# A transform run in smaller portions among matrix products, and an intermediate reordered by its copy

## The chip, the cores and the metric

The kernel runs on one core of a Trainium2 chip. The metric is the device time in microseconds (us). A kernel is run several times, and the median is quoted with the lowest and the highest time.

Engine names in the profile: PE is the tensor engine, PEld its weight loads, DVE the vector engine, ACT the scalar engine, POOL is GpSimd. In the traces below an engine takes its instructions in the order of the built program (run 1 shows ACT doing so). SBUF is the on-chip memory, and PSUM the memory into which PE writes.

## The reference, cut to what matters

The function is the forward and backward pass of a gated sum. One branch multiplies a two-dimensional real Fourier transform by complex weights, the other is a two-layer network with a squared ReLU. S is 2048, D is 1024, F is 3584, the data are bf16. It returns the output and eight gradients.

```python
X = rfft2(x.astype(float32)) * (w_r + 1j * w_i)
a = irfft2(X, s=(S, D)).astype(bfloat16)
h = einsum("bsd,df->bsf", x2, w1) + b1
r = where(h > 0, h, 0)
b = einsum("bsf,fd->bsd", r * r, w2) + b2
g = sigmoid((x * gate_w).sum(-1, keepdims=True))
out = g * a + (1 - g) * b          # jax.vjp(out)(grad_out) gives the eight gradients
```

## The kernel before

PE does everything large: 5376 products of 128x512 (six groups of 896) for the network, and the transforms, which are written as small matmuls. The transform of x and the transform of the output's gradient go through the same instructions as T = 0 and T = 1. The program is written as two generators, which a helper interleaves: for each 16-product accumulation of the weight gradients (`pw`; I call one such accumulation a *slot*) the transform generator is moved on by some steps. A step ends at a `yield`. What is left of the transform runs at one step per 28-product accumulation (`acc`) of the output stage. There DVE multiplies each finished accumulator with `go`, a loaded tile of the output's gradient, and sums the result into `bGo`; only then is the accumulator free again.

```python
def spread(main, side, per_main, start=0.0):
    due, done = start, 0
    for _ in main:
        due += per_main
        while done < due:
            next(side, None)
            done += 1
        yield
...
spec, grads = spectra(), mlp_grads()          # spectra: fft_mid, then fft_out
next(grads), next(grads)
todo = 1 + 6 * (S2 // 2) + NT                 # S2 // 2 = 8 pairs, NT = 16 tiles
for _ in spread(grads, spec, todo / (2.0 * FG * FGC * NH - 2)):
    pass
for _ in mlp_out():                           # 32 accumulations
    next(spec, None)
```

The middle of the transform (`fft_mid`) takes eight pairs of 128-point columns. A pair has two *units* (j) for each T: three matmuls, two into a PSUM buffer `px` and one into `pxs`; ACT copies `pxs` to SBUF as `common`; DVE adds it to both halves of `px`. `back` has the same form with `pv`, `pvs` and `v`. Each kind of PSUM buffer exists twice.

```python
def spectrum(fb, T, m, z, mats):
    ...                                       # DVE forms pm and sums
    for j in range(2):
        px = fps.tile([P, 2, H], FP32, name="px", tag="ps2", bufs=2)
        ps = tps.tile([P, H], FP32, name="pxs", tag="tr", bufs=2)
        mm(px[:, 0, :], lhsT=mats[:, j, 1, :], rhs=im, start=True, stop=True)
        mm(px[:, 1, :], lhsT=mats[:, j, 2, :], rhs=re, start=True, stop=True)
        mm(ps[:], lhsT=mats[:, j, 0, :], rhs=sums[:, j], start=True, stop=True)
        common = fb.tile([P, H], FP32, name="common", tag="common", bufs=2)
        nc.scalar.copy(out=common[:], in_=ps[:])
        by_l = lambda ap: ap.rearrange("p c (g i) -> p c i g", g=4)
        V(out=x[:, j, :, 0:H].rearrange("p c (i g) -> p c i g", g=4), in0=by_l(px[:]),
          in1=by_l(common[:]...).to_broadcast([P, 2, P, 4]), op=ALU.add)

# fft_mid, for each pair m
for T in range(2):
    xs.append(spectrum(fb, T, m, z[:, T], am))
    yield
real_columns(...)                             # small matmuls "sp"
for T in range(2):
    ...                                       # DVE: y = x * w, four products, combined
    yield
back(fb, m, y, ap)                            # all four units in one step
yield
...                                           # DVE: the gradient of the weights, gs
nc.scalar.mul(out=gw[:, :, :, 0:W1], in_=gs[:, :, :, 0:W1], mul=GS)
...
yield

# fft_out, for each of 32 tiles
...                                           # eight matmuls into pki
rt = fb.tile([P, 8, P], FDT, name="rt", tag="rt", bufs=2)
nc.scalar.copy(out=rt[:], in_=pk[:])
pu = fps.tile([P, 2, H], FP32, name="pui", tag="ps2", bufs=2)
column_stage(INV, pu, rt, ci)                 # eight matmuls into pui, from rt
...                                           # ACT copies pui, DVE finishes, store
yield 2
```

`spread` does not read the value that a generator yields, so `yield 2` is one step.

## Time and profile before

| | before |
|---|---|
| time, median of three | 1351.44 us (1350.59 to 1353.70) |
| span of the profiled execution | 1351.5 us |
| PE, DVE, ACT busy | 98%, 61%, 31% |
| PE idle, 450 to 800 us (transform among weight gradients) | 8.3 us |
| PE idle, 800 to 1060 us (last transform stage) | 3.3 us |
| PE idle, 1060 to 1100 us (start of the output stage) | 2.5 us |

The idle times are the length of a stretch less PE's busy time in it. They understate what is lost, because the end of a PE record is modelled: a record of 0.38 us stands for 0.216 us of issue. So in the tables further down I count another way, from the trace of one execution of each kernel: the distance between the starts of two neighbouring PE instructions, less N/2.4 ns + 2.5 ns for N columns (the prediction checks this spacing against the trace), for each distance that is over 30 ns too long. It is put down to the stage of the second instruction. Where a PE record is missing, the weight loads, whose records are all there, tell how many; this leaves an uncertainty of a few tenths of a us. This *lost PE time* is 11.6 us for the middle of the transform, 7.8 us for the last stage, and 2.6 us for the stop near 1075 us, plus 1.7 us for a stretch of half clock that follows it.

### The profile page before, as it was taken

The numbers are of one execution on the slowest core, as the hardware profiler recorded it, in microseconds if no ns is written. First come the engines' busy times: TensorE is split into PE (matmuls) and PEld (weight loads), VectorE is DVE, ScalarE is ACT, GpSimd is POOL, SyncE is SP. The second block draws the span as 40 slices with busy tenths as digits, with TensorE's granted clock in tenths as the row PEclk, the third lists the DMA queues.
The fourth block names the chain that finished last, engine by engine and source line by source line (L and its number), as shares of the span: only waits on it lengthen the run. The fifth ranks groups of instructions, "written<-read, shape, count | busy, mean of one in ns | idle before, by whom it ended". The sixth has DMA issues, their size and how long they took to land. (4 is left out here: it accounts for less than half of the span.)

```text
span 1351.5 us, 18838 instructions
## 1 busy us (share of the span) xinstructions
PE 1322.1 (98%) x7082; PEld 637.1 (47%) x7082; DVE 824.3 (61%) x1541; ACT 418.4 (31%) x658; POOL 299.3 (22%) x484
## 2 busy tenths in 40 slices
PE   7999999999999999999999999999999999999998
PEld 5644444444444444444444445454545444444443
DVE  7966667666565696769666782233856565642222
ACT  6854555555433323332233223343212000000000
POOL 0222223222322254443433222111101000000000
PEclk9999999999999999999999999999999999999999
DMA  8558778786778979889776548666888754653530
GB/s 280 188 182 250 255 229 259 247 252 225 226 235 242 287 226 196 202 234 200 206 167 194 141 126 276 208 220 233 214 224 230 203 169 133 193 165 94 155 102 24
DMA packets 217093, 273.31 MB, mean 202 GB/s; under 512 B 16988, under 2 KB 152170, under 8 KB 217002
## 3 DMA queue, kind: packets, MB, share of 16 engines
q1 hardware_dynamic: 181306, 153.84, 42.9%
q0 software_dynamic: 35696, 118.27, 27.0%
q8 instruction: 55, 0.90, 0.3%
q14 instruction: 36, 0.29, 0.1%
HBM read 147.25 MB, written 118.51 MB: 197 GB/s over the span
## 5 line engine op out<-in xcount | busy, mean ns | idle before, releaser
L617 PE MATMUL ph<-xT,w1g 128*128 128x512 bf16 x896 | 218.5, 381 | 2.0 <-ACT rT L619 1.7
L627 PE MATMUL pd<-dbT,w2T 128*128 128x512 bf16 x896 | 212.3, 379 | 1.2 <-DVE dhT L631 0.5
L904 PE MATMUL acc<-w,hblk 128*128 128x512 bf16 x896 | 199.8, 381 | 2.4 <-DVE bGo L906 2.4
L838 PE MATMUL pw<-grd,res 128*128 128x512 bf16 x896 | 201.6, 379 | 0.0
L821 PE MATMUL pw<-dbn,grp 128*128 128x512 bf16 x896 | 200.4, 379 | 0.0
L946 PE MATMUL accg<-w1Tr,hblk 128*128 128x512 bf16 x896 | 193.7, 379 | 0.0
L946 PEld LDWEIGHTS <-hblk 128*128 128x128 bf16 x896 | 87.6, 98 | 106.3 <-issue 0.9
L627 PEld LDWEIGHTS <-w2T 128*128 128x128 bf16 x896 | 87.2, 98 | 104.9 <-issue 1.6
L821 PEld LDWEIGHTS <-grp 128*128 128x128 bf16 x896 | 86.9, 98 | 105.4 <-issue 2.4
L904 PEld LDWEIGHTS <-hblk 128*128 128x128 bf16 x896 | 87.5, 98 | 103.3 <-issue 4.9
L838 PEld LDWEIGHTS <-res 128*128 128x128 bf16 x896 | 86.4, 98 | 101.3 <-issue 3.0
L617 PEld LDWEIGHTS <-w1g 128*128 128x128 bf16 x896 | 86.9, 98 | 99.5 <-issue 2.8
L619 ACT ACTIVATE rT<-ph,b1col 128x512 bf16<-128x512 f32 x112 | 77.0, 687 | 145.1 <-PE ph L617 145.0
L631 DVE SCALAR_TENSOR_TENSOR dhT<-pd,rT 128x512 bf16<-128x512 f32 x112 | 75.2, 671 | 65.9 <-PE pd L627 58.6
L951 DVE TENSOR_TENSOR gxo<-accg,g 128x512 bf16<-128x512 f32 x32 | 22.1, 690 | 108.1 <-PE accg L946 107.9
L736 DVE STREAM_TRANSPOSE stg<-h2T 128x512 int32<-128x512 int32 x56 | 39.8, 711 | 73.7 <-ACT h2T L620 73.7
L825 ACT CAST wo<-pw 128x512 bf16<-128x512 f32 x56 | 32.7, 585 | 156.6 <-PE pw L821 145.6
L833 POOL DMA_DIRECT2D out_dram<-wo x112 | 56.7, 514 | 84.8 <-ACT wo L825 79.1
L843 ACT CAST wo<-pw 128x512 bf16<-128x512 f32 x56 | 32.8, 586 | 125.7 <-PE pw L838 122.7
L620 ACT ACTIVATE h2T<-rT 128x512 bf16<-128x512 bf16 x112 | 70.6, 630 | 3.1
L743 DVE STREAM_TRANSPOSE stgd<-dhT 128x1024 bf16<-128x1024 bf16 x56 | 69.3, 1238 | 1.3
L496 DVE TENSOR_TENSOR ev<-e 128x256 f16<-128x256 f16 x32 | 9.3, 289 | 93.5 <-ACT e L493 93.4
(174 smaller groups left out, 1494.2 us busy)
## 6 DMA issues: line engine op xcount, KB each, us to landing
h2T_scr<-h2T POOLq DMA_DIRECT2D x28, 512.0 KB, 4.5
h_scr<-stg POOLq DMA_DIRECT2D x28, 512.0 KB, 7.0
dhT_scr<-dhT POOLq DMA_DIRECT2D x28, 512.0 KB, 8.0
dh_scr<-stgd POOLq DMA_DIRECT2D x28, 512.0 KB, 6.9
grp<-h_scr SPq DMA_DIRECT2D x112, 128.0 KB
grd<-dh_scr SPq DMA_DIRECT2D x112, 128.0 KB
hblk<-h2T_scr SPq DMA_DIRECT2D x8, 1792.0 KB
hblk<-dhT_scr SPq DMA_DIRECT2D x8, 1792.0 KB
```

What stands on the lines that cost most here:

```text
L617: mm(ph[:], lhsT=w1g[:, dc, fc % 2 * P : (fc % 2 + 1) * P], rhs=xT[:, dc, ss], start=(dc == 0), stop=(dc == DC - 1))
L619: nc.scalar.activation(rT[:], ph[:], ACT.Relu, bias=b1col[:, fc : fc + 1])
L620: nc.scalar.activation(h2T, rT[:], ACT.Square)
L627: mm(pd[:], lhsT=w_[:, ec // 2, ec % 2 :: 2], rhs=dbT[:, ec, ss], start=(ec == 0), stop=(ec == DC - 1),)
L631: return STT(out=dhT, in0=pd[:], scalar=2.0, in1=rT[:], op0=ALU.mult, op1=ALU.mult, accum_out=gb1part[:, fc, sb : sb + 1],)
L736: nc.vector.transpose(out=stg[:, :, c, :], in_=h2T[:, c, :].bitcast(I32).rearrange("p (b i) -> p b i", i=32))
L743: nc.vector.transpose(out=stg[:, :, :, c, :].rearrange("p b k i -> p k b i"), in_=dhT[:, c, :].rearrange("p (k b i) -> p k b i", b=4, i=32),)
L821: mm(pw[:], lhsT=cur[:, t // 2, 2 * fb_ * P + t % 2 : 2 * (fb_ + 1) * P : 2], rhs=dbn[:, t, hf * H : (hf + 1) * H], start=(t == 0), stop=( ...
L833: st(out=dst[q], in_=wo[32 * q : 32 * (q + 1), :])
L838: mm(pw[:], lhsT=xr[t][:, d_ * P : (d_ + 1) * P], rhs=cur[:, t], start=(t == 0), stop=(t == NT - 1),)
L904: mm(acc[:], lhsT=cur[:, fc, t2::2], rhs=w2[:, fc, cs], start=(fc == 0), stop=(fc == FC - 1))
L946: mm(acc[:], lhsT=cur[:, fc, t2::2], rhs=w1T[:, fc, 2 * hf : 2 * hf + 2, :], start=(fc == 0), stop=(fc == FC - 1),)
```

## The change

The intent is to give each engine time between portions, so that PE does not stand before a PSUM buffer that is still being emptied. Each unit becomes a step of its own, and each half of a last-stage tile. Since there are now more steps, the number of steps per slot is raised. And ACT writes `common` in the order in which DVE reads it, so DVE reads one of its two sources without hops.

```diff
-    def spectrum(fb, T, m, z, mats):
+    def spectrum(fb, m, z, mats, x):
@@
-            nc.scalar.copy(out=common[:], in_=ps[:])
-            by_l = lambda ap: ap.rearrange("p c (g i) -> p c i g", g=4)
+            nc.scalar.copy(
+                out=common[:].rearrange("p (i g) -> p i g", g=4), in_=ps[:].rearrange("p (g i) -> p i g", g=4)
+            )
             V(
-                out=x[:, j, :, 0:H].rearrange("p c (i g) -> p c i g", g=4), in0=by_l(px[:]),
-                in1=by_l(common[:].rearrange("p (o l) -> p o l", o=1)).to_broadcast([P, 2, P, 4]), op=ALU.add,
+                out=x[:, j, :, 0:H].rearrange("p c (i g) -> p c i g", g=4), in0=px[:].rearrange("p c (g i) -> p c i g", g=4),
+                in1=common[:].rearrange("p (o i g) -> p o i g", o=1, g=4).to_broadcast([P, 2, P, 4]), op=ALU.add,
             )
-        return x
+            yield
@@ back, at the end of each unit
+                yield
@@ fft_mid
-                xs.append(spectrum(fb, T, m, z[:, T], am))
-                yield
+                xs.append(fb.tile([P, 2, 2, LW], FDT, name=f"x{T}", tag=f"x{T}"))
+                yield from spectrum(fb, m, z[:, T], am, xs[T])
@@
-            back(fb, m, y, ap)
+            yield from back(fb, m, y, ap)
@@ fft_out
                 nc.scalar.copy(out=rt[:], in_=pk[:])
+                yield
                 pu = fps.tile([P, 2, H], FP32, name="pui", tag="ps2", bufs=2)
@@
-    todo = 1 + 6 * (S2 // 2) + NT
+    todo = 1 + 12 * (S2 // 2) + 2 * NT
```

Lines move by one or two: the products of the weight gradients are L821 and L838 before, L823 and L840 after; the output products L904 before, L906 after; the copy and the add of `spectrum` are L328 and L330 before, L327 and L330 after. In `back` the copy and the add are L381 and L382 in both.

More of the change, by code (lines that the diff above doesn't have):

```diff
@@ L318, in spectrum @@
         V(out=sums[:], in0=re_, in1=im_, op=ALU.add)
-        x = fb.tile([P, 2, 2, LW], FDT, name=f"x{T}", tag=f"x{T}")
         for j in range(2):
```

## The prediction

> **What bounds the kernel now.** I read the page's busy shares first, then busy time by stage, then what TensorE (PE) waits for, then single gaps in order of time, then the vector engine's (DVE) groups and the chain that ended last.
>
> ```profile
> PE 1322.1 (98%) x7082; PEld 637.1 (47%) x7082; DVE 824.3 (61%) x1541; ACT 418.4 (31%) x658; POOL 299.3 (22%) x484
> ```
>
> PE is busy for 98% of the span, so the time can only fall by what PE loses between its instructions. By stage (transforms among the weight gradients, 450 to 800; last transform stage, 800 to 1060; a gap, 1060 to 1100; the rest):
>
> ```profile
> 450.00:800.00 350.00, 341.73 (x1621) 153.17 (x1619) 263.94 (x340) 99.74 (x158) 128.80 (x231) 1.00 0.76 194
> 800.00:1060.00 260.00, 256.71 (x1505) 130.16 (x1504) 131.44 (x411) 84.98 (x100) 41.98 (x76) 1.00 0.77 224
> 1060.00:1100.00 40.00, 37.55 (x167) 16.63 (x166) 24.49 (x48) 0.00 (x0) 2.16 (x4) 0.96 0.76 209
> 1100.00:1350.00 250.00, 247.54 (x1143) 111.33 (x1140) 101.60 (x140) 0.00 (x0) 12.19 (x21) 1.00 0.43 128
> ```
>
> The columns are stretch, length, then busy us of PE, PE's weight loads, DVE, ACT and GpSimd, granted clock, DMA share, GB/s. PE is idle 8.3, 3.3 and 2.5 us in the three stretches that the change touches. DVE is at 75% in the first and blocks nothing for long. What PE waited for:
>
> ```profile
> PE pvs L379 <- ACT common L381: 3.6, 3, 1.2
> PE pv L377 <- DVE v L382: 2.8, 4, 0.7
> PE acc L904 <- DVE bGo L906: 2.4, 1, 2.4
> ...
> PE px L325 <- DVE pm L311: 1.6, 2, 1.2
> PE pxs L326 <- DVE sums L318: 0.8, 2, 0.4
> ```
>
> The first two are waits for a PSUM buffer: four units (two T, two j) of the backward transform stand almost together in PE's order, with two buffers of each kind. The third unit needs the buffers that the first unit's copy and add have yet to free:
>
> ```profile
> 677.84 0.38 PE L379 MATMUL pvs<-ysums,apmat 128*128 128x512 f16 x1
> 678.06 0.38 PE L821 MATMUL pw<-dbn,grp 128*128 128x512 bf16 x1
> 679.68 0.38 PE L379 MATMUL pvs<-ysums,apmat 128*128 128x512 f16 x1 [1.24 <-ACT common L381]
> ```
>
> Starts of dense 512-column matmuls are 0.216 us apart (39 in 8.58 us elsewhere, one record being 0.38), so a start at 678.28 was due and 1.40 us went, of which the record shows 1.24. Each gap hides 0.38 - 0.216 = 0.16 us in this way. The eleven waits of the transform stage (3+4+2+2) sum to 8.8 us idle, so to 8.8 + 11 x 0.16 = 10.6 us of PE time.
>
> In the last stage each of the 32 tiles has a shorter gap of the same kind:
>
> ```profile
> 860.32 0.61 PE L487 MATMUL pki<-ki,r 128*128 128x128 f16 x8
> 860.76 1.67 PE L838 MATMUL pw<-grd,res 128*128 128x512 bf16 x7
> 862.50 0.91 PE L281 MATMUL pui<-ci,rt 128*128 128x256 f16 x8
> ```
>
> Seven products from 860.76 end their issue at 862.27; the second half starts at 862.50. So 0.23 us per tile goes to waiting for ACT's 1.02 us copy of the first half. The group's row has only 2.6 us of idle time for 32 tiles, since 0.16 of each gap is hidden: 2.6 + 32 x 0.16 = 7.7 us, and 32 x 0.24 gives the same.
>
> The third loss is in the chain that ended last:
>
> ```profile
> 1059.38 14.41 DMA go<-in_grad_out_dram
> 1073.79 0.02 issue
> 1073.82 1.23 DVE junk L894
> ```
>
> A 256 KB load of go, issued just behind a 1792 KB block load, holds DVE for 12.5 us; four accumulators fill and PE stops for 2.45 us. After that the clock is halved for a window: eight matmuls at twice 0.21 us in the timeline, another 1.7 us. Sum 4.3 us with what is hidden.
>
> **What the Trainium skill says.** (1) "TensorE: Matmul & The Clock Gate", § Back-to-back issue gap: N/2.4 + 2.5 ns, 216 ns for 512 columns. The trace has 0.216 us. (2) "Perfetto Trace Analysis", § Tensor Engine Instruction (MATMUL, LD_WEIGHTS): the end of a PE record is estimated from the instruction's size. The trace agrees: records of 0.38 us start 0.216 us apart, which is why I add 0.16 to each gap. (3) "Vector Engine (DVE) Microarchitecture Reference", § 5.2 Measured stream behaviour: a stream that hops at every element costs 1.73 ns per column when one source hops, 1.76 when both do, 1.054 when none does. The rows here agree:
>
> ```profile
> L330 DVE TENSOR_TENSOR x<-px,common 128x1024 f16<-128x1024 f32 x32 | 60.2, 1918 | 5.3 <-ACT common L328 5.3
> L382 DVE TENSOR_TENSOR v<-pv,common 128x1024 f16<-128x1024 f32 x32 | 37.3, 1214 | 3.0 <-ACT common L381 3.0
> L542 DVE COPY dbT<-pt 128x1024 bf16<-128x1024 bf16 x16 | 18.6, 1219 | 0.0
> ```
>
> L330 and L382 do the same add on the same size, and differ in that both inputs of L330 are read with a hop at every element: (1918 - 1214)/1024 = 0.69 ns per column. (4) The first page again, § Part 1: The HAM clock gate: after an idle window of about 3.4 us PE drops to half rate. Here 2.45 us of idle was enough, by the trace.
>
> **The change part by part.** Matmuls, operands and sizes stay: 7082 PE instructions before and after. Three things move.
>
> *The copy puts the common product in order.* It takes one of the two hops of L330 away; the other, on PSUM, stays. Read for SBUF, the skill's table then promises nothing (1.73 against 1.76). But L542 reads PSUM with a hop at every element and takes 1219 ns for 1024, as L382 does without hops, and ACT's half of the same transposes takes 1024 ns against 1015 for copies without hops. So I guess, at 7 to 3, that hops in PSUM are free: L330 falls from 1918 to about 1215 ns, 32 x 0.70 = 22.5 us of DVE time, and the copy stays near 585 ns. None of it is on PE's path as such; it only brings x earlier and frees px 0.7 us earlier.
>
> *Units in smaller portions.* In the changed program's order as built, 16 products (16 x 0.216 = 3.46 us) stand between most units, where before none stood between the two of a T, and none or one to four between those of the backward transform. A unit's buffers come free about 0.1 + 0.59 (copy) + 1.21 (add) = 1.9 us after its last matmul, so the seven buffer waits (6.4 + 7 x 0.16 = 7.5 us) should go. The four input waits (2.4 + 0.6 = 3.1 us) are not of that kind: DVE had not yet formed pm or sums. About half should go, since DVE is ahead. On the other side the backward transform now starts 32 products (6.9 us) after the small real-column matmuls instead of 48 or more (10.4). Before its third matmul can start, DVE has two L364, four multiplications at 1.23, four combinations at 0.69 (two of them after ysums) and one ysums at 0.69: 0.3 + 4.9 + 1.4 + 0.7 = 7.3 us, 7.0 with overlaps. That is level with the 7.3 us that PE takes to get there, so I add 8 x 0.15 = 1.2 us. Net: 7.5 + 1.5 - 1.2 = 7.8 us saved.
>
> *Halves of a last-stage tile.* In the built order 13 of the 32 tiles still have only 5 or 7 products between halves (13 x 0.24 = 3.1 us stay), 15 have 16 or 28 (nothing lost), and four stand in two clusters where a first half is followed by its second half at once, or nearly: two lose the whole copy, 1.3 us each, two some 0.4. That leaves 6.5 of 7.7 us: 1.2 us saved. The last 16 tiles now spread over all 32 output accumulations instead of the first 16.
>
> *The gap at 1075* is an accident of order: a small load behind a large one. In the changed order the pairs of block load and go are still there, so it may vanish, move or double. I take half its cost as gone in the mean: 2 us saved, plus or minus 4.
>
> Sum: 7.8 + 1.2 + 2 = 11 us, less 0.5 for a possible wait of the first last-stage tile, whose load now has 56 products after the last small matmuls instead of 80. Prediction: 1351.4 - 10.5 = 1341 us.
>
> **The rivals.** (a) *The waits only move.* DVE is in order and at 75% in this stage; a portion that comes too early for DVE turns a buffer wait into an input wait. For it: sums and pm waits exist already, and the 7.3 against 7.0 us above. It would give some 1347 us. Against it: DVE loses 22 us of work if the hop is free. (b) *DVE was the true limit of the stage*, so that 22 us of it come through. Against it: PE is idle only 8.3 us there, so 1351 - 23 = 1328 would be the very best, with every gap of all three kinds gone. (c) *The output stage gets worse*: transforms spread through it put DVE further behind, and PE stops at every block load, three or four times 4 us: 1352 to 1356. For it: DVE already waited for go four times, 21.4 us in all. Against it: only one of these reached PE.
>
> **Range and chances.** Everything the change can touch is 10.6 + 7.7 + 4.3 = 22.6 us, 1.7% of the time, so faster by over 2% is nearly shut out; slower by over 2% needs 27 us of new stops. Range 1335 to 1348.
>
> **What would show it.** PE idle at 450 to 800 down from 8.3 to about 2 us, with the waits for common and v gone from the list; L330 near 1215 ns and its copy near 590 (wrong: over 1800, or a copy of over 900); about 13 tiles with the 0.24 us gap and four in two clusters in the last stage; the gap at 1075 seen or not. A DVE input wait (pm, sums, ysums) of over 5 us in all would prove rival (a), several waits for bGo rival (c).

## The result, and the profile after

| | before | after |
|---|---|---|
| median | 1351.07 us | 1343.35 us |
| lowest to highest, four runs each | 1350.59 to 1353.70 | 1340.22 to 1344.87 |
| span of the profiled execution | 1351.5 us | 1340.5 us |

A ratio here is the mean time of one kernel's fast runs over the mean time of the other's in the same rounds, so it is not quite the ratio of the medians. It is 0.9936 (95% interval 0.9913 to 0.9959): within 2%, and inside the predicted range. The gain is 0.0064 x 1351 = 8.6 us. The two profiled executions are 11.0 us apart, since that of the kernel before was among its slower ones (1353.24 us). So sums from the two traces should be a little larger than the gain in time.

The engine shares of the kernel after, in the order busy time, share of the span, instructions:

```profile
PE 1311.1 (98%) x6974; PEld 638.2 (48%) x7082; DVE 802.1 (60%) x1541; ACT 419.9 (31%) x658; POOL 295.7 (22%) x484
```

DVE lost 22.2 us of work. Of PE's matmuls, 108 have no record here, so PE's idle time is overstated by some of those. The three stretches of the kernel after (columns as in the prediction):

```profile
450.00:800.00 350.00, 344.44 (x1620) 155.30 (x1641) 251.33 (x348) 103.20 (x162) 126.98 (x233) 1.00 0.77 197
800.00:1060.00 260.00, 255.54 (x1435) 128.96 (x1448) 113.74 (x341) 67.65 (x82) 36.96 (x67) 1.00 0.79 223
1060.00:1100.00 40.00, 39.03 (x210) 19.24 (x212) 31.81 (x85) 7.46 (x8) 3.78 (x7) 1.00 0.72 223
```

PE is idle 5.6, 4.5 and 1.0 us, against 8.3, 3.3 and 2.5 before. What PE of the kernel after waited for (total us, times, longest):

```profile
PE pui L281 <- ACT rt L490: 3.8, 5, 1.2
PE pxs L325 <- DVE sums L318: 3.1, 3, 2.4
...
PE pv L377 <- DVE y L452: 0.6, 2, 0.4
...
PE pvs L379 <- DVE ysums L373: 0.5, 2, 0.2
```

The waits for `common`, `v`, `pm` and `bGo` are gone. Those for `rt` have grown into the list, and one wait for `sums` of 2.4 us is new. DVE's two adds in the kernel after (busy us, mean ns, then what DVE waited for):

```profile
L330 DVE TENSOR_TENSOR x<-px,common 128x1024 f16<-128x1024 f32 x32 | 38.8, 1221 | 44.2 <-ACT common L327 44.2
L382 DVE TENSOR_TENSOR v<-pv,common 128x1024 f16<-128x1024 f32 x32 | 38.7, 1219 | 4.2 <-ACT common L381 4.2
```

The add of `spectrum` now takes what the add of `back` takes, though its PSUM source is still read with a hop at every element. ACT's copy L327 takes 587 ns, against 586 before.

One of the two clusters of last-stage tiles that the prediction names, from PE's timeline after (start, length, then the instructions and the wait before them):

```profile
1028.34 0.61 PE L488 MATMUL pki<-ki,r 128*128 128x128 f16 x8
1030.11 0.91 PE L281 MATMUL pui<-ci,rt 128*128 128x256 f16 x8 [1.16 <-ACT rt L490]
1030.86 0.61 PE L488 MATMUL pki<-ki,r 128*128 128x128 f16 x8
1031.30 1.46 PE L906 MATMUL acc<-w,hblk 128*128 128x512 bf16 x5
1033.08 0.91 PE L281 MATMUL pui<-ci,rt 128*128 128x256 f16 x8 [0.32 <-ACT rt L490]
```

The second half follows the first at once and waits for the whole copy of it, 1.16 + 0.16 = 1.3 us; the next tile has six products between (one has no record), and loses 0.5 us. The stop near 1075 in the kernel before, and then the same place in the kernel after, a stream without a wait:

```profile
1077.87 7.46 PE L904 MATMUL acc<-w,hblk 128*128 128x512 bf16 x26 [2.45 <-DVE bGo L906]
```

```profile
1075.22 4.48 PE L906 MATMUL acc<-w,hblk 128*128 128x512 bf16 x20
```

DVE waited 3.5 us in two waits for go, against 21.4 us in four. By lost PE time the middle went from 11.6 to 5.9 us, the last stage from 7.8 to 7.4, and the stop with its half clock from 4.3 to 0: 5.7 + 0.4 + 4.3 = 10.4 of the 11.0 us between the two spans; most of the rest lies before 450 us, where the programs are the same. So *where* the time came from is accounted for. *Which part of the change* brought it is another question, and two traces cannot answer it.

### The profile page after: what moved, and what is told of

It reads as the page before. It is cut to its first block, busy times and chain, and to the rows that moved or that the text cites. A ratio compares the mean times of both kernels' runs of the same rounds, so it can differ in the third digit from the quotient of the medians.

```text
span 1340.5 us, 18698 instructions
## 1 busy us (share of the span) xinstructions
PE 1311.1 (98%) x6974; PEld 638.2 (48%) x7082; DVE 802.1 (60%) x1541; ACT 419.9 (31%) x658; POOL 295.7 (22%) x484
## 5 line engine op out<-in xcount | busy, mean ns | idle before, releaser
L619 PE MATMUL ph<-xT,w1g 128*128 128x512 bf16 x866 | 214.5, 381 | 2.9 <-ACT rT L621 1.2
L840 PE MATMUL pw<-grd,res 128*128 128x512 bf16 x896 | 201.7, 379 | 0.0
L823 PE MATMUL pw<-dbn,grp 128*128 128x512 bf16 x875 | 199.9, 379 | 1.2 <-issue 0.2
L906 PE MATMUL acc<-w,hblk 128*128 128x512 bf16 x874 | 196.3, 379 | 1.2
L823 PEld LDWEIGHTS <-grp 128*128 128x128 bf16 x896 | 86.8, 98 | 103.0 <-issue 0.9
L906 PEld LDWEIGHTS <-hblk 128*128 128x128 bf16 x896 | 87.1, 98 | 99.4
L840 PEld LDWEIGHTS <-res 128*128 128x128 bf16 x896 | 86.5, 98 | 99.3 <-issue 1.1
L490 ACT CAST rt<-pki 128x1024 f16<-128x1024 f32 x32 | 32.4, 1014 | 126.2 <-PE pki L488 126.0
```

The source lines that it names most:

```text
L619: mm(ph[:], lhsT=w1g[:, dc, fc % 2 * P : (fc % 2 + 1) * P], rhs=xT[:, dc, ss], start=(dc == 0), stop=(dc == DC - 1))
L823: mm(pw[:], lhsT=cur[:, t // 2, 2 * fb_ * P + t % 2 : 2 * (fb_ + 1) * P : 2], rhs=dbn[:, t, hf * H : (hf + 1) * H], start=(t == 0), stop=( ...
L840: mm(pw[:], lhsT=xr[t][:, d_ * P : (d_ + 1) * P], rhs=cur[:, t], start=(t == 0), stop=(t == NT - 1),)
L906: mm(acc[:], lhsT=cur[:, fc, t2::2], rhs=w2[:, fc, cs], start=(fc == 0), stop=(fc == FC - 1))
```

## The experiments

The change has four parts that can be separated: the reordering copy, the units as steps, the halves as steps, and the *spread*, that is, the pace of steps per slot and the last 16 tiles over 32 output accumulations instead of 16. Every kernel below gave a correct result. "Before" is timed on the same chip in the same rounds.

### 1. The copy alone

```diff
--- before
-            nc.scalar.copy(out=common[:], in_=ps[:])
+            nc.scalar.copy(
+                out=common[:].rearrange("p (i g) -> p i g", g=4), in_=ps[:].rearrange("p (g i) -> p i g", g=4)
+            )
             V( ... in1=common[:].rearrange("p (o i g) -> p o i g", o=1, g=4).to_broadcast([P, 2, P, 4]), op=ALU.add)
```

> Only the reordering copy; portions and order in time as before. Theory (PE's own waits decide, DVE time is off its path): L330 falls from 1918 to about 1221 ns, which frees some 22 us of DVE, but the time falls by at most 1.5 us (1349.5 to 1351), with the waits of the backward transform for common and v (6.4 us) still there. Rival (the DVE time of the stage was what counted): a fall of 5 us or more, 1346 or less.

Measured: 1347.62 us (1347.05 to 1348.41) against 1351.13; ratio 0.9973 (0.9960 to 0.9987), so 0.0027 x 1351 = 3.6 us. That is more than my theory allowed (1.5) and less than its rival asked (5). The prediction had said that nothing of the copy is on PE's path. The trace of the kernel before shows what it missed. ACT, just before the wait for `common` that the prediction displays:

```profile
676.76 1.92 ACT L464 ACTIVATE gw<-gs 128x2052 bf16<-128x2052 f16 x1 [2.62 <-DVE gs L462]
678.58 0.57 ACT L825 CAST wo<-pw 128x512 bf16<-128x512 f32 x1
679.04 1.08 ACT L381 COPY common<-pvs 128x512 f32<-128x512 f32 x2
```

`pvs` was finished by about 677.4, but its copy began at 679.04. ACT takes its work in order; ahead of the copy stood the scaling of the same pair's weight gradient (`gw`; in the text of the program it comes after `back`, so the build's scheduler has moved it ahead), which had waited 2.62 us for DVE's `gs` and then took 1.92 us. So DVE's lateness does reach PE, through ACT's queue. The same place with the copy alone:

```profile
674.09 1.92 ACT L465 ACTIVATE gw<-gs 128x2052 bf16<-128x2052 f16 x1 [1.50 <-DVE gs L463]
675.91 0.57 ACT L826 CAST wo<-pw 128x512 bf16<-128x512 f32 x1
676.38 1.08 ACT L382 COPY common<-pvs 128x512 f32<-128x512 f32 x2
```

There `pv`'s first matmul starts at 675.21 instead of 676.76 (before, then with the copy):

```profile
676.76 0.38 PE L377 MATMUL pv<-y,apmat 128*128 128x512 f16 x1
```

```profile
675.21 0.38 PE L378 MATMUL pv<-y,apmat 128*128 128x512 f16 x1
```

So from that start to the copy it is 1.17 us instead of 2.28. PE's waits for `common` and `pm` are gone from the list; that for `v` stays (2.8 us), and the stop before `bGo` is 1.8 us.

### 2. The portions without the copy

The changed kernel with the copy and the add of before put back.

```diff
--- after
-            nc.scalar.copy(
-                out=common[:].rearrange("p (i g) -> p i g", g=4), in_=ps[:].rearrange("p (g i) -> p i g", g=4)
-            )
+            nc.scalar.copy(out=common[:], in_=ps[:])
             V( ... as before ...)
```

> The portions without the reordering copy: L330 stays at 1918 ns. Theory (waits for PSUM buffers in PE's order): nearly the whole gain remains, 1342 to 1345, and the waits for v and common are gone; a little more waiting for pm and sums than in the changed kernel, 1 to 2 us. Rival (DVE time): 1349 or more.

Measured: 1354.52 us (1352.44 to 1354.79); ratio 1.0018 (1.0005 to 1.0030). It is slower than before, so the theory of a gain of 6 us or more from the portions by themselves fell. What PE of this kernel waited for:

```profile
PE pxs L325 <- DVE sums L318: 4.4, 4, 3.0
...
PE pv L376 <- DVE y L451: 3.2, 2, 2.9
PE pvs L378 <- DVE ysums L372: 2.9, 4, 0.9
PE px L324 <- DVE pm L311: 2.3, 2, 1.2
```

Of the waits for a buffer in the middle only one of 0.2 us is left, and the stop for `bGo` is gone; but there are 12.8 us of waits for what DVE has yet to produce. With twelve steps per pair, 32 products and not 48 or more stand between the small matmuls and `back`, and DVE, which still spends 1921 ns on each add, isn't through. This is rival (a) of the prediction. With the copy the same program takes 1343.35 us: between portions, the copy is worth (1.0018 - 0.9936) x 1351 = 11 us, three times what it is worth alone.

### 3 and 4. Units only, halves only: the pace was not held

One removes the `yield` between the halves from the changed kernel, the other adds just that `yield` to the kernel before; each with the step count to match.

```diff
--- after, for units only
-                yield                            # between rt and pui
-    todo = 1 + 12 * (S2 // 2) + 2 * NT
+    todo = 1 + 12 * (S2 // 2) + NT
--- before, for halves only
+                yield                            # between rt and pui
-    todo = 1 + 6 * (S2 // 2) + NT
+    todo = 1 + 6 * (S2 // 2) + 2 * NT
```

> Units in portions and the reordering copy, last-stage tiles whole. If the stop of 2.45 us behind the late go load in the output stage was removed by the halves (transforms spread over all of that stage), it comes back here: a wait for bGo of 2 us or more, a half-clock window, and 1345 to 1346. If it went for another reason (luck of order), it stays away and the time is 1341 to 1343. In both cases idle PE time at 450 to 800 is as in the changed kernel, 4 to 6 us instead of 8.3.

> Only the last-stage halves, units as before, no reordering copy. Theory: the 8 us of PE idle at 450 to 800 stay. In the order as built some nine tiles keep a short distance between their halves, two of them none, so about 4.7 us of the 7.7 us in that stage stay. If the spreading also removes the stop behind the go load (4.3 us): 1344 to 1345. If not: 1348 to 1349.

Measured: units only 1349.36 us (1348.24 to 1352.37), ratio 0.9987 (0.9975 to 1.0000); halves only 1355.21 us (1353.30 to 1355.66), ratio 1.0023 (1.0011 to 1.0036). Neither tells what it was meant to tell. In the first there are 97 steps in the middle of 113, so the middle of the transform takes some 94 of the 110 slots instead of some 83, and the last stage is pressed into what is left: lost PE time is 1.6 us in the middle, but 13.7 us in the last stage. In the second there are 49 of 81, the middle is pressed into some 66 slots, and loses some 20 us. The lesson is in the design: a `yield` sets where work may go *and* what share of the slots it takes. The next ones hold the pace by adding empty steps.

### 5. The gradient's scaling moved off ACT, first try

A test of the path through ACT. On the kernel before, `gw` is scaled on GpSimd.

```diff
--- before
-            nc.scalar.mul(out=gw[:, :, :, 0:W1], in_=gs[:, :, :, 0:W1], mul=GS)
+            nc.gpsimd.tensor_scalar(out=gw[:, :, :, 0:W1], in0=gs[:, :, :, 0:W1], scalar1=GS, scalar2=None, op0=ALU.mult)
```

> The kernel before, with only the scaling of the weight gradient (the 1.92 us copy gw on ACT) moved to GpSimd; L330 stays at 1918 ns. New theory: ACT works in order, gw waits there for DVE's late gs and holds back the common copy behind it, and that copy was what PE waited for; so the wait of pvs for common (3.6 us) goes though DVE is as slow as before, and the time falls by 2.5 to 4 us, to 1347 to 1348.5. Rival (the copy's gain came from DVE's own results being earlier): the wait stays, 1350 or more.

Measured: 1364.93 us (1364.01 to 1365.81), ratio 1.0096 (1.0081 to 1.0112). The wait for `common` did vanish, but a larger one took its place. GpSimd needs 5.44 us for what ACT does in 1.92; DVE's small scaling of the edge columns of `gw` waits for it, 16.7 us in all, and PE's wait for `v` is 14.6 us. Three of these stops last 4.0 us each, and in the trace the clock is halved around each of them, 17 us in all. As a test of size it is worthless.

### 6 and 7. Units, and halves, at the pace of the change

For units, the changed kernel with whole tiles, and two steps at the end of each. For halves, the kernel before with the copy and the halves, and every step of the middle doubled by an empty one, so that units stay together.

```diff
--- after, for units with the spread
-                yield                            # between rt and pui
+                yield 2                          # a second one at the end of a tile
--- before with the copy, for halves with the spread
+                yield                            # one more after each step of fft_mid (four places)
+                yield                            # between rt and pui
-    todo = 1 + 6 * (S2 // 2) + NT
+    todo = 1 + 12 * (S2 // 2) + 2 * NT
```

> The changed kernel with the last-stage tiles whole again, but each handed on as two steps, so that pace and spread over the output stage are those of the changed kernel. If spreading the tiles over all of the output stage is what removed the stop behind the go load: no wait for bGo, 1343 to 1345. If cutting the tiles in halves did it: the wait of about 2 us is back, 1346 to 1348.

> Reordering copy and last-stage halves at the pace of the changed kernel, but the units of the middle stage together as before. If the portions of the middle stage give nothing once the copy is in order (the first copy-only run already lost as little there as the changed kernel): 1342 to 1344.5, like the changed kernel. If they do give something: 1346 to 1348.

Measured: units with copy and spread 1346.26 us (1344.91 to 1348.14), ratio 0.9960 (0.9947 to 0.9972); halves with copy and spread 1344.93 us (1342.59 to 1345.34), ratio 0.9944 (0.9932 to 0.9957). So by the ratios leaving out the units costs about 1 us (0.9944 against 0.9936), and leaving out the halves about 3 us (0.9960). The halves come out as worth more than the units, the reverse of the prediction, though the intervals of the two runs overlap a little. In both, the stop before `bGo` is gone.

### 8. The last stage as a pipeline

The clusters show that a step between halves is no promise of distance. Here the first half of tile n+1 is put before the second half of tile n, in a step of its own, so there is always a whole step between a tile's halves.

```diff
--- after
+        rows_part(*tiles_[0])                    # load, pki, copy to rt
+        yield
+        for n in range(2 * NT):
+            if n + 1 < 2 * NT:
+                rows_part(*tiles_[n + 1])
+                yield
+            columns_part(*tiles_[n])             # pui, copy, DVE, store
+            yield
```

> The changed kernel with the last stage in a pipeline: first half of tile n+1, then second half of tile n. If the 6 us lost there are waits of a second half for ACT's copy of its own first half: the waits of pui for rt (3.8 us) go, and the time is 1337 to 1340. If those waits only turn into others (PSUM buffers, loads of r): 1342 to 1345.

Measured: 1338.65 us (1338.07 to 1339.27), ratio 0.9901 (0.9888 to 0.9915): 4.7 us better than the change, and its slowest run is faster than the fastest of the change (1340.22 us). The last stage of this kernel:

```profile
800.00:1060.00 260.00, 257.76 (x1463) 132.44 (x1477) 120.13 (x353) 70.23 (x85) 36.96 (x67) 1.00 0.81 227
```

PE is busy for 257.76 us of it against 255.54 in the kernel after; no wait of `pui` for `rt` is left, though four waits for a PSUM buffer (1.4 us) are new, and lost PE time there falls from 7.4 to 2.6 us, by as much as the time.

### 9. The gradient's scaling moved off ACT, second try

The same test as in 5, on DVE, which needs 0.70 us for it. The copy and the add of L330 stay as before (1922 ns).

```diff
--- before
-            nc.scalar.mul(out=gw[:, :, :, 0:W1], in_=gs[:, :, :, 0:W1], mul=GS)
+            nc.vector.tensor_scalar(out=gw[:, :, :, 0:W1], in0=gs[:, :, :, 0:W1], scalar1=GS, scalar2=None, op0=ALU.mult)
```

> The kernel before, with the scaling gw moved from ACT to DVE ([...]some 0.7 us instead of 1.92 on ACT; on GpSimd it took 5.44 us and DVE waited for it); L330 stays at 1918 ns. If ACT's order (gw ahead of common) is how DVE's lateness reached PE: the wait of pvs for common (3.6 us) goes and nothing takes its place, 1347 to 1349. If the lateness reaches PE in another way: 1350 to 1353, with waits of pv for v or of pvs for ysums grown instead.

Measured: 1348.60 us (1347.72 to 1349.50), ratio 0.9973 (0.9960 to 0.9987), the same gain as the copy alone, with DVE's work *larger* than before. In ACT's and PE's timelines of this kernel, at the same place:

```profile
678.50 1.23 ACT L381 COPY common<-pvs 128x512 f32<-128x512 f32 x2
```

```profile
678.95 0.38 PE L821 MATMUL pw<-dbn,grp 128*128 128x512 bf16 x1
679.17 0.38 PE L379 MATMUL pvs<-ysums,apmat 128*128 128x512 f16 x1
679.38 0.59 PE L821 MATMUL pw<-dbn,grp 128*128 128x512 bf16 x2
```

The copy comes as soon as its `pvs` is there, and the third unit follows at the dense distance of 0.22 us, where before it waited 1.24 us. Lost PE time in the middle is some 7 us instead of 11.6. The waits for `v` (3.1 us) and `bGo` (2.7 us) stay. So the path is shown from both ends: it goes away when DVE is earlier, and when ACT has nothing of DVE's to wait for.

### 10 and 11. Combined, and more buffers for the stores

The pipeline of 8 with the scaling of 9; and then four buffers instead of two for `wo`, the tile that ACT fills from `pw` and a DMA stores. The second is a test of the wait for `sums`. In the kernel after, ACT and then PE, near 610 us:

```profile
609.58 0.59 ACT L827 CAST wo<-pw 128x512 bf16<-128x512 f32 x1 [6.75 <-DMA out_dram<-wo]
610.06 0.59 ACT L327 COPY common<-pxs 128x512 f32<-128x512 f32 x1
```

```profile
612.57 0.39 PE L325 MATMUL pxs<-sums,amat 128*128 128x512 f16 x1 [2.38 <-DVE sums L318]
```

ACT stands 6.75 us before a store that has yet to free `wo`; `common` is behind it, DVE's add behind that, and `sums` behind the add. PE is the last of the row.

```diff
--- 10: the pipelined kernel of 8
-            nc.scalar.mul(out=gw[:, :, :, 0:W1], in_=gs[:, :, :, 0:W1], mul=GS)
+            nc.vector.tensor_scalar(out=gw[:, :, :, 0:W1], in0=gs[:, :, :, 0:W1], scalar1=GS, scalar2=None, op0=ALU.mult)
--- 11: kernel 10
-                    wo = wb.tile([P, D], BF16, name="wo2", tag="wo2", bufs=2)
+                    wo = wb.tile([P, D], BF16, name="wo2", tag="wo2", bufs=4)
```

> The changed kernel with the last stage in a pipeline (1338.65 in the job before), and gw on DVE. In that kernel no wait of PE for common was left, so little remains to gain: 1337 to 1339. If DVE's further 5.5 us count: 1340 or more.

> As e10, with four buffers instead of two for the output rows wo of the first weight gradient. In the changed kernel's trace ACT stood 10.9 us for stores of wo (two times), and common copies behind it made PE wait once for sums (2.4 us). If that is the cause of this wait: 1 to 2.5 us less than e10 and no wait for sums over 1 us. If not: the same as e10.

Measured: 1337.36 us (1336.12 to 1337.91), ratio 0.9888 (0.9875 to 0.9902); and 1335.67 us (1334.82 to 1335.69), ratio 0.9876 (0.9862 to 0.9889). PE's wait for `sums` in kernel 10, and then in kernel 11:

```profile
PE pxs L325 <- DVE sums L318: 3.2, 2, 2.8
```

```profile
PE pxs L325 <- DVE sums L318: 0.4, 1, 0.4
```

The long one is gone, and with it ACT's long stand at this place (7.16 us in kernel 10, 2.87 in kernel 11, where it waits for `pw` as in other slots), and lost PE time in the middle falls from 5.8 to 3.0 us. The intervals of 8, 10 and 11 overlap from one to the next, so the times alone do not prove the single steps. Kernel 11 beats both kernels: 16 to 17 us under the kernel before and 8 us under the change.

### 12. The copy and the spread, no portion

The last part that had not been alone: the kernel before with the copy, all units and tiles whole, each step doubled by an empty one, and the step count of the change.

```diff
--- before with the copy
+                yield                            # one more after each step of fft_mid (four places)
+                yield 2                          # a second one at the end of a tile
-    todo = 1 + 6 * (S2 // 2) + NT
+    todo = 1 + 12 * (S2 // 2) + 2 * NT
```

> The reordering copy and only the pace of the changed kernel: units together, last-stage tiles whole, each tile handed on as two steps, so that the last 16 spread over all 32 output accumulations. If spreading alone removes the stop behind the go load: no wait of acc for bGo, no half-clock window, 1344.5 to 1346.5, against 1347.6 for the copy alone. If it needs the halves: the wait of about 2 us stays, 1347 to 1349.

Measured: 1348.08 us (1345.99 to 1348.92), ratio 0.9971 (0.9957 to 0.9984), where the copy alone has 0.9973. The stop before `bGo` is gone, but the last stage loses 11.0 us instead of 7.8, and the middle 7.1 instead of 5.7. One of its gaps, from PE's timeline of this kernel:

```profile
1032.71 0.91 PE L281 MATMUL pui<-ci,rt 128*128 128x256 f16 x8 [1.16 <-ACT rt L494]
```

So the spread by itself nets nothing that these runs resolve: it removes one loss and adds another.

### The parts together

| copy | spread | halves | units | run | ratio | lost PE time: middle, last stage, stop (us) |
|---|---|---|---|---|---|---|
| | | | | before | 1 | 11.6, 7.8, 2.6 (and 1.7 of half clock) |
| x | | | | 1 | 0.9973 | 5.7, 7.8, 1.9 |
| x | x | | | 12 | 0.9971 | 7.1, 11.0, 0 |
| x | x | | x | 6 | 0.9960 | 3.8, 10.6, 0 |
| x | x | x | | 7 | 0.9944 | 7.1, 7.4, 0 |
| x | x | x | x | after | 0.9936 | 5.9, 7.4, 0 |
| | x | x | x | 2 | 1.0018 | 15.7 (and 1.6 of half clock), 7.2, 0 |

Read as steps of 1351 us: the copy 3.6 us; the spread 0.3; the halves 3.6 (12 to 7) or 3.2 (6 to after); the units 1.5 (12 to 6) or 1.1 (7 to after). The path by way of 7 gives 3.6 + 0.3 + 3.6 + 1.1 = 8.6 us, as it must. These are worths in this order, with the copy first: the other three parts without it (run 2) lose time. In the traces the halves take 3.2 to 3.6 us off the last stage, as much as they take off the time, and the units take 3.3 us off the middle (12 to 6), or 1.2 (7 to after, where the wait for `sums` of 2.4 us is new). The copy's interval excludes 1. For the halves, the intervals of runs 12 and 7 meet only at 0.9957. For the units the intervals of the pairs overlap (0.9957 to 0.9984 against 0.9947 to 0.9972), so their gain is likely, and small, and not proved.

## Why the prediction was right or wrong

The time was right: 1341 predicted, 1343.35 measured. The account of it was wrong in two of its four terms, and the errors cancelled: too much for the units (7.8 us against some 1.1), nothing for the copy (against 3.6), and too little for the halves and their spread. That the sum came out is luck.

**The copy, "None of it is on PE's path as such": wrong.** It gave 3.6 us alone and 11 us between the portions. I looked at what PE waited for, found ACT and not DVE as the engine that the largest wait names, and stopped there. ACT was itself waiting for DVE, with another instruction, one place ahead in its order. Runs 1 and 9 show this path; the trace of before had it, in the ACT timeline shown under run 1. The size of the effect on DVE was right: 1918 to 1221 ns (about 1215 predicted), 32 x 0.70 = 22.3 us, and the copy at 587 ns. The guess at 7 to 3, that a hop in PSUM is free, was borne out.

**Units, 7.8 us: mis-sized.** In these runs they gave 1.1 to 1.5 us. The mechanism, buffer waits going when units stand apart, is right as far as the list of waits goes: none is left in run 6 or after, and 0.2 us in run 2. Three of the seven buffer waits, however, were those for `common`, which the copy had removed already; the `pm` waits as well. And what was gained was partly spent again: on inputs (the `y` and `ysums` waits, 1.1 us), and on the wait for `sums` at 612 us, which comes from the stores of `wo` (run 11). The term should have been computed on the kernel *with* the copy, in which the middle loses 5.7 us and not 10.6. Without the copy the portions lose time, as rival (a) said and run 2 showed. The estimate of 7.3 us for PE against 7.0 us for DVE was the right comparison; it was as close as it looked, and the copy is what keeps DVE ahead.

**Halves, 1.2 us: the pattern right, the size off.** The prediction left 6.5 us in the last stage, and 7.4 us are lost there. The pattern is the one that was read from the built order: thirteen tiles with a short gap, fifteen with none, and two clusters, in each of which one tile loses 1.3 us. But the second tile of a cluster loses 0.5 and 0.9 us instead of 0.4, and one of the thirteen 0.5 instead of 0.24. The loss before is 7.8 us (7.7 predicted), so across the whole change the last stage gained 0.4 us. But the spread, which the prediction put into the same paragraph without a cost, by itself raises the loss to 11.0 us, and the halves bring it down again. Against that, they are worth 3.2 to 3.6 us.

**The gap at 1075, 2 us saved, plus or minus 4: within its range.** It is gone, with its half clock: 4.3 us in the two traces. In the times it is probably less, since not every execution seems to have the half clock: of the 36 timed executions of the kernel before that ran beside the experiments, 19 have a granted clock of 1.000 on record and 17 one of 0.998 or 0.999, and the former are 1.3 us faster in the mean. The gap is present in all five kernels that leave the last tiles to the first accumulations (before, 1, 3, 5, 9), and absent in the nine others (after, 2, 4, 6, 7, 8, 10, 11, 12). So it belongs to the spread, and not to the copy, the units or the halves. What within the spread makes DVE wait 3.5 us for go instead of 21.4 was not isolated; this stays open.

**The first last-stage tile, 0.5 us:** no such wait came: the list of the kernel after has none. Run 6 has one wait of 0.6 us for a load of `r`, but at 1069 us, at a late tile.

**The rivals.** (a) is false for the change and true without its copy. (b), DVE as the real limit, has more in it than I gave it, since DVE's time reaches PE through ACT, but the gain stayed far from 23 us. (c), an output stage with several stops for `bGo`, was not seen.

**The checks.** PE idle in the first stretch "down from 8.3 to about 2 us" was wrong: it is 5.6 us, part of it missing records. The other marks, the waits for `common` and `v` gone and no input wait of over 5 us in all, held.

## What to carry to other kernels

When a wait names an engine that is mostly idle, read that engine's own timeline just before it: in-order queues carry the lateness of a third engine to the bottleneck. Smaller portions change a wait for a buffer into a wait for an input unless the producer is ahead, so make the producer faster first, and put a fixed distance between dependent halves (run 8) rather than a mere chance of one. In a study of parts, hold the pace of the interleaving; runs 3 and 4 measured the pace instead of the part.

## What the Trainium skill lacked or had wrong

- "Vector Engine (DVE) Microarchitecture Reference", § 5.2 Measured stream behaviour, measures hops in SBUF and has no row for PSUM. Here an add with a PSUM source that hops at every element (512 bytes), beside a contiguous SBUF source, takes 1221 ns for 1024 columns, as against 1219 ns without the hop. With the hop also in the SBUF source it is 1918 ns. So the hop in PSUM was free.
- No page that I read has a figure for ACT's copy from PSUM with such hops: 587 ns for 512 columns, 586 without.
- "TensorE: Matmul & The Clock Gate", § Part 1: The HAM clock gate, names an idle window of about 3.4 us and does not say how much of it must be idle. Stops of 2.45 us (before) and 2.94 us (run 2) were followed by half clock; stops of 1.78, 2.32 and 2.66 us (runs 1, 3, 9) were not, and neither was one of 3.00 us in run 2, near 620 us. So the length of the stop alone did not decide.
- The same page, § Back-to-back issue gap, says that its formula over-counts in a stream with weight loads, where it gives some 131 ns for 512 columns. In such a stream here the starts are 216 ns apart, which is the formula.
- "GPSIMD Engine Reference", § 4.1 Engine selection, calls one-input operations on GpSimd roughly line-rate. A scaling of 2052 columns from f16 to bf16 took 5.44 us there, 1.92 us on ACT and 0.70 us on DVE (runs 5, before, 9).
